# Attention ahead of an MoE and an MLP on one core: another order of issue, second-batch logits in column groups, a mask matmul of 96 columns

## The chip, the cores and the metric

One core of one Trainium2 chip runs the whole program in one launch. The metric is device time in microseconds (us); the time before is the median of three runs. Engines are named as the profile names them: PE (TensorE matmul), PEld (its weight loads), DVE (VectorE), ACT (ScalarE), POOL (GpSimd), SP (SyncE, which issues the loads and stores).

## The reference, cut to what matters

```
B, H, S, D = 2, 8, 768, 64;  block, window = 32, 16;  nb = 24
k_sum = max over each 32 keys;  v_sum = mean over each 32 values
scores = [ q k^T / 8, masked to |i - j| < 16 ;  q k_sum^T / 8 + log(32) ]      # 768 + 24 columns
x = softmax(scores) @ [v ; v_sum]                      # -> x: 1536 tokens x 512
logits = x @ w_gate                                    # 8 experts, 192 tokens each, greedy by the largest logit
out[tokens of e] = relu(x[tokens of e] @ w1[e]) @ w2[e]
h = out @ w_in;  result = relu(h)^2 @ w_out
```

## The kernel before

The program has two parts. `attention` (lines 61 to 413) computes x and the router's logits, and it also does the first round of the routing; `moe` (from line 588) does the other seven rounds, the eight experts and the MLP.

**Units.** Attention is cut into twelve units of four (head pair, 128 query tokens) slots. Units 0 to 5 are the first batch; the four slots of a unit are four neighbouring blocks there. Units 6 to 11 are the second batch: a unit is one block of 128 tokens with all four head pairs, so that the 512 features of its tokens are complete. Each unit passes through the same steps: `sc` (two mask matmuls that write a PSUM tile `S` through the identity, L246, and sixteen score matmuls on 64 x 64 pieces of the array, L250), `sm` (row maximum, DVE, L259), `sb` (exponentials, ACT, L263), `tr` (PE transposes of the probabilities, L270, and the copy of them), `pv` (sixteen matmuls with the values, L284), `pn` (division by the sum, DVE, L294 to L299), `st` (store of x), `xt` (PE transposes of x, L321, and the copy), `la` and `lb` (logits, below). Ahead of the units stand, for each batch and head pair, the steps `lk`, `lq`, `lv` (loads), `rk`, `rq` (copies of rows), `pk`, `pq` (PE transposes, L193, with the copy), `pb` and `pw` (block maxima and key windows), and `va`, `vb`, `vc` (sums of the values; L110 and L119 on PE).

**Logits.** In the first batch `la` issues four matmuls, one into each group of 32 columns of the array (L342: 32 weight columns, 128 moving columns each), ACT copies the result (`lt`, L345), and `lb` adds the four groups with one full matmul (L353). In the second batch `la` accumulates four full matmuls with x as the weights and 8 moving columns (L336), DVE copies the 8 columns to `L9` (L337), and there is no `lb`.

**Routing in attention.** `to`, `ro`, `ch` take the largest logit of some blocks, transpose it into a row and make the one-hot choice; `g` compares (DVE, L562, 36 of them, 256 to 1536 columns wide), and `cn` counts with matmuls on 32 columns of the array (L574). `cl` is the last count and `cd` reads the result (L583, L585). The first instruction of `moe` on PE is the transpose at L734; after it come matmuls on the identity that nobody reads (L676), then L772.

**What sets the order.** Every step is a token of the table `ORDER` (lines 31 to 54), and line 410 walks through it: a token's instructions are put at the end of the lists of their engines. Each engine works through its own list in that order and waits where an operand is not there. A last digit 0, 1 or 2 in `rk`, `rq`, `pk`, `pq`, `tr`, `xt`, `vc`, `pw` names the engine that copies (ACT, DVE, POOL). `w.n` issues n matmuls of 512 columns on the identity that nobody reads (L370). All PE steps but `sc`, `pv` and `cn` write tiles `T` of one pool of three PSUM buffers, so the fourth `T` waits for the copy of the first.

**Form of the array.** A PE instruction uses the full array (L193, L246, L270, L321, L336, L353, L370, L526), 64 x 64 pieces (L250), 64 columns (L284) or 32 columns (L110, L119, L342, L574). "A change of form" below is a neighbouring pair of PE instructions with different forms.

Of the kernel before, what the change touches and what calls it, by code (L numbers as in the profile page):

```python
# [25 lines left out]
WIN = 96  # L26
KW = WIN + NB
# [1 line left out]

PART = ((0, 6), (6, 8), (8, 10), (10, 12))  # L30
ORDER = """
w.8 rk.0.0.0 pk.0.0.0.0 lk.0.3 rk.0.1.1 rq.0.0.1 pk.0.0.1.0 w.2 pk.0.1.0.0 pq.0.0.0.0 lq.1.3 pb.0.0 rq.0.1.1
pw.0.0.2 lq.0.2 pk.0.1.1.0 pq.0.0.1.1 sc.0 lk.0.2 pb.0.1 rk.0.3.2 sm.0.0 rq.1.3.0 pq.0.1.0.1 lv.0.0 sm.0.1
pk.0.3.0.1 pk.0.3.1.1 pq.1.3.0.1 pw.0.1.2 rq.0.2.2 sb.0.0 w.2 sc.1 rk.0.2.2 sm.1.0 pq.0.1.1.1 sb.0.1 sb.1.0 tr.0.1.0
pq.1.3.1.0 pb.0.3 sm.1.1 lk.1.0 pk.0.2.0.0 pw.0.3.2 sc.2 sb.1.1 sm.2.1 lk.1.2 tr.0.0.1 lq.0.3 pk.0.2.1.0 tr.1.0.0
sm.2.0 pb.0.2 sb.2.0 tr.1.1.1 rk.1.0.1 pq.0.2.0.0 va.0.0 pq.0.2.1.1 sb.2.1 pw.0.2.2 rq.0.3.2 lq.1.1 tr.2.0.1 vb.0.0
pk.1.0.0.1 lk.1.3 rk.1.2.0 vc.0.0.0.1 sc.3 lq.1.0 lk.1.1 rq.1.1.2 vc.0.0.1.1 tr.2.1.0 sm.3.0 sm.3.1 pk.1.0.1.0
pq.0.3.0.1 sb.3.0 rq.1.0.2 pb.1.0 pv.0 pk.1.2.0.0 rk.1.3.2 pn.0 lv.0.1 lq.1.2 sb.3.1 pk.1.2.1.1 sc.4 pq.1.1.0.0
tr.3.1.0 sm.4.0 sm.4.1 sb.4.0 pv.1 rk.1.1.2 pw.1.0.2 pq.0.3.1.0 pq.1.1.1.0 lw pk.1.1.0.0 sc.5 pk.1.1.1.0 pn.1 pb.1.2
sm.5.1 pw.1.2.2 pq.1.0.0.1 xt.0.1 sm.5.0 sb.4.1 pk.1.3.0.0 pk.1.3.1.0 pv.2 pb.1.1 pb.1.3 xt.1.0 st.1 pw.1.3.2 sb.5.0  # L40
tr.4.1.1 va.0.1 la.0 la.1 rq.1.2.1 pq.1.2.0.0 pn.2 st.0 pw.1.1.2 lb.0 vb.0.1 vc.0.1.1.2 lb.1 vc.0.1.0.1 tr.3.0.0
lv.1.0 lv.1.1 sb.5.1 xt.2.1 sc.6 la.2 sm.6.0 st.2 sb.6.0 tr.5.1.0 tr.4.0.0 lb.2 pv.3 pn.3 sc.7 sm.7.0 xt.3.1
tr.5.0.1 sb.7.0 va.1.0 sm.6.1 la.3 pv.5 lb.3 pn.5 sb.6.1 sm.7.1 pq.1.2.1.0 st.5 pq.1.0.1.1 sc.8 op xt.5.1 sb.7.1
sm.8.0 pv.4 sb.8.0 tr.6.1.1 la.5 pn.4 va.1.1 lb.5 vb.1.0 sm.8.1 vb.1.1 tr.6.0.0 xt.4.1 vc.1.1.0.1 sc.9 sb.8.1 sm.9.0
st.3 la.4 tr.7.0.0 sm.9.1 vc.1.0.0.2 tr.8.0.0 lb.4 pv.6 sb.9.0 to.0 pn.6 vc.1.0.1.2 st.4 vc.1.1.1.2 ro.0 tr.7.1.0
ch.0.0 st.6 sb.9.1 sc.10 pv.7 ch.0.1 ch.0.2 ch.0.3 xt.6.0 g.0.0 g.0.1 cn.0 tr.8.1.0 g.0.2 tr.9.1.0 sm.10.1 pn.7
g.0.3 la.6 sm.10.0 xt.7.0 sb.10.0 g.0.4 pv.8 tr.9.0.0 pn.8 la.7 cn.1 sb.10.1 g.0.5 to.1 tr.10.0.0 ch.1.0 ch.1.1 pv.9
pn.9 ro.1 st.7 sc.11 g.1.0 g.1.1 sm.11.0 xt.9.0 xt.8.0 tr.10.1.0 cn.2 sm.11.1 g.1.2 sb.11.1 g.1.3 g.1.4 la.9 g.1.5
sb.11.0 g.1.6 cn.3 la.8 pv.10 cn.4 ch.1.2 to.2 ch.1.3 st.8 ro.2 pn.10 tr.11.1.0 cn.5 tr.11.0.0 st.9 cn.6 g.1.7
ch.2.0 xt.10.0 g.2.0 cn.7 g.2.1 cn.8 g.2.2 pv.11 g.2.3 pn.11 la.10 st.10 ch.2.1 g.2.4 cn.9 g.2.5 g.2.6 cn.10 g.2.7  # L50
xt.11.0 cn.11 g.2.8 la.11 cn.12 ch.2.2 cn.13 cn.14 to.3 ro.3 cn.15 cn.16 cn.17 g.2.9 cn.18 ch.2.3 g.3.0 cn.19 g.3.1
cn.20 g.3.2 ch.3.0 ch.3.1 cn.21 qu g.3.3 g.3.4 g.3.5 cn.22 g.3.6 cn.23 cn.24 ch.3.2 cn.25 cn.26 cn.27 g.3.7 g.3.8
ch.3.3 g.3.9 st.11 cn.28 cn.29 cn.30 cn.31 g.3.10 cn.32 cn.33 cn.34 g.3.11 cl cd
"""


# [4 lines left out]
def attention(ctx, tc, nc, q, k, v, wg, x_dram, L9, identf, identb, late=None):  # L61

    const = ctx.enter_context(tc.tile_pool(name="a_const", bufs=1))
# [1059 lines left out]
```

## Time and profile before

| | us |
|---|---|
| median of three runs (603.37 to 604.30) | 603.57 |
| the profiled execution, its own time | 604.21 |
| its span on the core | 602.2 |
| busy in the span: PE / DVE / ACT / POOL | 584.5 / 357.5 / 194.3 / 79.9 |
| attention: first mask matmul on PE to the end of `cd` | 11.58 to 106.65 |

A row of the timeline gives the start, the busy time of a merged run of instructions, the engine, the line, the operands, the count and, in brackets, the idle time ahead of it and what ended it. Busy time of PE overlaps between neighbours, so the cost of a group of matmuls is read as the distance from its start to the next group's start. A matmul on float32 operands leaves two records, a transpose one. PEclk is the granted clock of PE, 1.00 for 2.4 GHz and 0.50 for 1.2 GHz.

### The profile page before, as it was taken

What the parts mean: (1) busy time and instruction counts of PE and PEld (TensorE: products, weight loads), DVE (VectorE), ACT (ScalarE), POOL (GpSimd) and SP (SyncE); (2) the same over time, 40 slices, a digit from 0 to 9 for tenths busy, and PEclk for the clock granted to TensorE, in tenths of its full rate; (3) what the DMA queues carried; (4) which work ended last, traced back from release to release, by engine and by line L of the source; (5) the groups of instructions that cost most, each with busy time, mean ns of one, the idle gap of its engine ahead of it and who ended that gap; (6) DMA issues with size and microseconds to landing.
All of it is one profiled execution on the core that took longest, in us unless ns stands there. A gap on an engine that the chain in (4) does not pass through costs nothing.

```text
span 602.2 us, 10554 instructions
## 1 busy us (share of the span) xinstructions
PE 584.5 (97%) x4118; PEld 479.5 (80%) x4118; DVE 357.5 (59%) x830; ACT 194.3 (32%) x416; POOL 79.9 (13%) x132
## 2 busy tenths in 40 slices
PE   6999998899999999999999999999999999999996
PEld 4677785478879788799999888888888888888884
DVE  6896867679888797955566688873322222322221
ACT  4775663213223142312222333332312222222221
POOL 7354300202030220211000000000300000300002
PEclk8999988899999999999999999999999999999998
DMA  9995111452726548269853254320100000100001
GB/s 242 246 201 113 55 53 38 165 212 94 282 83 227 208 150 289 91 224 308 307 200 115 96 174 136 130 86 0 71 0 2 1 0 1 70 2 0 1 0 70
DMA packets 55393, 71.34 MB, mean 118 GB/s; under 512 B 21296, under 2 KB 32560, under 8 KB 55344
## 3 DMA queue, kind: packets, MB, share of 16 engines
q1 hardware_dynamic: 53360, 64.38, 33.9%
q0 software_dynamic: 1984, 6.29, 3.1%
q8 instruction: 32, 0.52, 0.4%
q14 instruction: 17, 0.14, 0.1%
HBM read 64.37 MB, written 6.29 MB: 117 GB/s over the span
## 4 chain that ended last, share of the span: by engine, by line
PE 79%; issue 13%; DVE 3%; DMA 2%; POOL 1%; ACT 1%; SPq 0%; POOLq 0%; DVEq 0%; ACTq 0%
PE pg L1023 16%; PE ph L919 15%; PE ph L936 15%; PE ph L1049 11%; PE px L1049 4%; PE cnt L574 3%; PE O L284 2%; PE T L193 2%; PE T L270 2%; PE S L250 2%; POOL out_dram L1059 1%; PE ms L526 1%; DMA rawk<-in_k_dram 1%; PE T L321 1%; PE T L110 1%
## 5 line engine op out<-in xcount | busy, mean ns | idle before, releaser
L919 PE MATMUL ph<-xt,w 128*128 128x192 f32 x512 | 92.2, 332 | 0.0
L936 PE MATMUL ph<-ht,w 128*128 128x192 f32 x512 | 91.4, 331 | 0.0
L936 PEld LDWEIGHTS ph<-ht,w 128*128 128x128 f32 x512 | 82.6, 190 | 6.8 <-issue 6.7
L562 DVE TENSOR_SCALAR G<-mrow,m 128x1536 bf16<-128x1536 f32 (+4 forms) x108 | 84.5, 836 | 4.9 <-PE cnt L574 2.7
L919 PEld LDWEIGHTS ph<-xt,w 128*128 128x128 f32 x512 | 82.4, 190 | 5.0 <-issue 4.3
L1023 PE MATMUL pg<-yhi,w 128*128 128x512 f32 x192 | 59.4, 391 | 0.0
L1027 DVE TENSOR_TENSOR xa<-xa 128x512 f32<-128x512 f32 x24 | 16.6, 692 | 58.2 <-ACT xa L1026 57.7
L1027 DVE TENSOR_TENSOR xb<-xb 128x512 f32<-128x512 f32 x24 | 16.6, 691 | 54.4 <-ACT xb L1026 54.4
L1059 POOL DMA_INDIRECT out_dram<-f,sci x6 | 5.9, 979 | 301.5 <-DVE f L1057 300.9
L1023 PEld LDWEIGHTS pg<-yhi,w 128*128 128x128 f32 x192 | 36.1, 188 | 7.7
L1023 PE MATMUL pg<-ylo,w 128*128 128x512 f32 x96 | 37.5, 391 | 0.0
L1049 PE MATMUL ph<-w,xt 128*128 128x512 f32 x144 | 35.3, 389 | 0.0
L1026 ACT ACTIVATE xa<-pg 128x512 f32<-128x512 f32 x24 | 14.2, 592 | 59.3 <-PE pg L1023 59.3
L924 ACT ACTIVATE ht<-ph 128x384 f32<-128x384 f32 x32 | 15.7, 491 | 52.7 <-PE ph L919 50.4
L1026 ACT ACTIVATE xb<-pg 128x512 f32<-128x512 f32 x24 | 14.2, 594 | 55.7 <-PE pg L1023 55.7
L1049 PEld LDWEIGHTS ph<-w,xt 128*128 128x128 f32 x144 | 27.0, 188 | 5.6
L1023 PE MATMUL pg<-yhi,w2b 128*128 128x512 f32 x96 | 30.2, 395 | 0.0
L1023 PE MATMUL pg<-yhi,w2a 128*128 128x512 f32 x96 | 29.7, 391 | 0.0
L263 ACT ACTIVATE P<-S,nm 128x120 f32<-128x120 f32 x96 | 26.6, 372 | 8.8 <-DVE nm L259 8.3
L631 DVE TENSOR_SCALAR f<-raw 128x512 int32<-128x512 int32 x32 | 13.5, 423 | 18.6 <-DMA raw<-in_moe_w_in_dram 10.7
L942 ACT ACTIVATE yhi<-ph 128x384 fp32r<-128x384 f32 x16 | 7.8, 488 | 51.3 <-PE ph L936 40.9
L635 DVE SCALAR_TENSOR_TENSOR f<-raw,f 128x512 int32<-128x512 int32 x32 | 22.2, 693 | 1.0
(234 smaller groups left out, 1005.0 us busy)
## 6 DMA issues: line engine op xcount, KB each, us to landing
w<-in_moe_w_dram SPq DMA_DIRECT2D x64, 512.0 KB, 6.0
raw<-in_moe_w_in_dram SPq DMA_DIRECT2D x16, 512.0 KB, 3.7
raw<-in_moe_w_out_dram SPq DMA_DIRECT2D x16, 512.0 KB, 3.2
vw<-in_v_dram SPq DMA_DIRECT2D x16, 240.0 KB, 5.6
rawk<-in_k_dram SPq DMA_DIRECT2D x8, 384.0 KB, 7.0
rawq<-in_q_dram SPq DMA_DIRECT2D x8, 384.0 KB, 7.1
x_dram<-x SPq DMA_DIRECT2D x10, 256.0 KB, 2.2
vw<-in_v_dram SPq DMA_DIRECT2D x8, 80.0 KB, 4.8
```

The source lines that it names most:

```text
L263: nc.scalar.activation(P[u][:, hh, i], SS[u][hh][:, i], AF.Exp, bias=NM[u][:, hh, i:i + 1])
L562: self.nc.vector.tensor_scalar(t[:, used:used + w], self.mrow[:, 128 * j0:128 * j1], self.m[:, c:c + 1], CS, op0=OP.is_le, op1=OP.mult)
L574: self.nc.tensor.matmul(self.cnt[32 * g:32 * g + 32, 128 * (lo - 3 * g):128 * (hi - 3 * g)], self.o[:, c, :], t[:, 128 * (lo - j0):128 * ( ...
L631: nc.vector.tensor_scalar(fi, raw[:, :, 1], 3, 0x3FFFFFF8, op0=OP.logical_shift_left, op1=OP.bitwise_and)
L635: nc.vector.scalar_tensor_tensor(fi, raw[:, :, 0], 29, fi, op0=OP.logical_shift_right, op1=OP.bitwise_or)
L919: nc.tensor.matmul(ps[:, j, 0:CAP], w[:, k, 128 * (f % 4):128 * (f % 4) + 128], d["xt"][:, k, :], start=(k == 0), stop=(k == 3), skip_grou ...
L924: nc.scalar.activation(d["ht"][:, f0:f0 + 2, :], ps[:, :, 0:CAP], AF.Relu)
L936: nc.tensor.matmul(ps[:, j, 0:CAP], w[:, f % 4, 128 * dd:128 * dd + 128], d["ht"][:, f, :], start=(f == 0), stop=(f == 7), skip_group_chec ...
L1023: nc.tensor.matmul(ps, a[:, k, fs], b[:, k, js], start=(n == 0), stop=(n == 11))
L1026: nc.scalar.activation(r, ps, AF.Relu)
L1027: nc.vector.tensor_tensor(r, r, r, op=OP.mult)
L1049: nc.tensor.matmul(PO[j][t], a[:, 128 * t:128 * t + 128], b[:, f % 4, :], start=(f == 0 and n == 0), stop=(f == 15 and n == 2))
```

## The change

The order table is replaced. It has the same tokens but for these: six `lb` are added (units 6 to 11), the fillers `w` go from 8, 2, 2 to 8, 2, 3, 3, 3, 3, 4, and 42 of the tokens with an engine digit copy on another engine. The second batch's `la` becomes that of the first batch, and a new branch in `lb` sums the four groups into 8 columns with one full matmul. The mask loses its last 24 columns, which were zero, and the mask matmul writes 4 x 96 columns of S where it wrote 480.

```diff
-w.8 rk.0.0.0 pk.0.0.0.0 lk.0.3 rk.0.1.1 rq.0.0.1 pk.0.0.1.0 w.2 pk.0.1.0.0 pq.0.0.0.0 lq.1.3 pb.0.0 rq.0.1.1
...
+w.8 rq.0.0.1 rk.0.0.0 lq.0.2 pk.0.0.0.0 pk.0.0.1.1 lk.0.2 rk.0.1.0 pb.0.0 lk.0.3 w.2 pq.0.0.0.0 w.3 pk.0.1.0.0
...
-    mask = const.tile([128, 12, KW], BF, name="mask")
-    nc.vector.tensor_copy(mask, ma[:, None, :].to_broadcast([128, 12, KW]))
+    mask = const.tile([128, 12, WIN], BF, name="mask")
+    nc.vector.tensor_copy(mask, ma[:, None, :].to_broadcast([128, 12, WIN]))
...
-            m = mask[:, c:c + 1, :].to_broadcast([128, 4, KW])
+            m = mask[:, c:c + 1, :].to_broadcast([128, 4, WIN])
...
-            nc.tensor.matmul(ss[hh], identb, m, start=True, stop=False, skip_group_check=True)
+            nc.tensor.matmul(ss[hh][:, :, 0:WIN], identb, m, start=True, stop=False, skip_group_check=True)
...
-        if b == 1:
-
-            ps = pT.tile([128, E], F32, name="T")
-            for a in range(4):
-                nc.tensor.matmul(ps, xt[:, a, :], wgs[:, a, 0:E], start=a == 0, stop=a == 3)
-            nc.vector.tensor_copy(L9[:, 6 + slots[0][1], 0:E], ps)
-            return
...
         ps = pT.tile([128, 4, E], F32, name="T")
+        if b == 1:
+
+            nc.tensor.matmul(ps[:, 0, :], lt, esel24[:, 0:E], start=True, stop=True)
+            nc.vector.tensor_copy(L9[:, 6 + slots[0][1], 0:E], ps[:, 0, :])
+            return
```

Line numbers of the changed kernel are one higher between the order table and the mask and two lower from the second part of `logit_b` on. Three places show how the lists move.

On PE in the second batch, before: the end of a unit's probabilities (`P`), logits (L336), the next unit's x, its values (`O`) and its logits.

```order
L270 MATMUL T<-identf,P 120x128 x8
L336 MATMUL T<-wgs,xt 128x8 x4
L321 MATMUL T<-identf,x 128x128 x4
L284 MATMUL O<-vw,PT 64x65 x16
L270 MATMUL T<-identf,P 120x128 x4
L336 MATMUL T<-wgs,xt 128x8 x4
```

The same two units (6 and 7) in the changed kernel, where L335 is the first half of the logits, L348 the second half, and L246 and L250 the scores of the last unit.

```order
L321 MATMUL T<-identf,x 128x128 x4
L284 MATMUL O<-vw,PT 64x65 x16
L335 MATMUL T<-xt,wgs 32x128 x8
L270 MATMUL T<-identf,P 120x128 x4
L246 LDWEIGHTS identb
L246 MATMUL S<-mask,identb 128x4x96
L246 LDWEIGHTS identb
L246 MATMUL S<-mask,identb 128x4x96
L250 MATMUL S<-kw,qt 64x120 x16
L348 MATMUL T<-esel_165,lt 128x8 x2
L284 MATMUL O<-vw,PT 64x65 x16
```

Two units' logits stand side by side now, their second halves six groups later, between groups of the same form.

On DVE at the start, before: the first rows of k and q (`rk`, `rq`), then the block maxima `ks` of the first head pair.

```order
L184 COPY rk<-rawk 128x768
L184 COPY rq<-rawq 128x768
L209 TENSOR_REDUCE ks<-kt_107 128x24
L184 COPY rq<-rawq 128x768
L226 TENSOR_SCALAR qt<-T 128x384
```

In the changed kernel the q rows of the first head pair come first and the copy of its keys follows; the k rows of the second head pair are copied on ACT.

```order
L184 COPY rq<-rawq 128x768
L202 COPY kt_107<-T 128x384
L209 TENSOR_REDUCE ks<-kt_107 128x24
L202 COPY kt_108<-T 128x384
L209 TENSOR_REDUCE ks<-kt_108 128x24
```

The first block maxima no longer stand behind two copies of rows, the first of which needs the third load.

On PE at the end of attention, before: the last count (L574), the transpose that opens `moe` (L734) and its first filler.

```order
L574 LDWEIGHTS O_0_1103
L574 MATMUL S<-G,O_0_1103 32x384
L734 MATMUL ms<-identf,tm 128x128
L676 LDWEIGHTS identb
L676 MATMUL ph<-identb 128x512
```

The same place in the changed kernel.

```order
L572 LDWEIGHTS O_0_1240
L572 MATMUL S<-G,O_0_1240 32x384
L368 LDWEIGHTS identb
L368 MATMUL T<-identb 128x512
L368 LDWEIGHTS identb
L368 MATMUL T<-identb 128x512
L368 LDWEIGHTS identb
L368 MATMUL T<-identb 128x512
L368 LDWEIGHTS identb
L368 MATMUL T<-identb 128x512
L732 MATMUL ms<-identf,tm 128x128
```

Four fillers (`w.4`) stand between the last count and the transpose; three more groups of three stand among the counts ahead of them. From L588 on (the part `moe`) the lists of all five engines are the same in both kernels.

## Rows read from the trace of the kernel before

**Rows 1.** Four stretches: length; busy us of PE, PEld, DVE, ACT, POOL; PEclk; DMA share; GB/s

```profile
12.00:87.00 75.00, 71.75 (x1148) 54.78 (x1146) 60.52 (x132) 49.51 (x150) 28.17 (x43) 1.00 0.66 141
87.00:91.00 4.00, 4.00 (x44) 3.16 (x43) 2.33 (x12) 0.95 (x4) 0.20 (x1) 0.57 0.01 2
98.00:107.00 9.00, 6.04 (x50) 2.67 (x45) 7.15 (x21) 2.34 (x5) 0.45 (x2) 0.69 0.00 0
107.00:111.00 4.00, 4.00 (x13) 1.53 (x12) 2.10 (x14) 0.00 (x0) 0.00 (x0) 0.50 0.19 55
```

**Rows 2.** Timeline of PE: logits by full matmuls (L336), and the clock's fall

```profile
75.60 0.96 PE L336 MATMUL T<-wgs,xt 128*128 128x8 f32 x8
76.41 0.63 PE L321 MATMUL T<-identf,x 128*128 128x128 f32 x4
...
86.11 1.06 PE L336 MATMUL T<-wgs,xt 128*128 128x8 f32 x8
87.09 1.95 PE L284 MATMUL O<-vw,PT 120*64 120x65 f32 x32
```

**Rows 3.** Timeline of PE: transposes, the logits in column groups (L342, L353), values

```profile
48.75 0.43 PE L342 MATMUL T<-xt,wgs 128*32 128x128 f32 x8 [0.97 <-DVE xt L324]
49.11 1.09 PE L270 MATMUL T<-identf,P 128*120 128x128 f32 x8
50.03 0.31 PE L353 MATMUL T<-esel,lt 128*128 128x32 f32 x2
50.27 1.15 PE L284 MATMUL O<-vw,PT 120*64 120x65 f32 x32
```

**Rows 4.** Timeline of ACT in the second batch: exponentials (L263) and what stands behind them

```profile
85.32 2.13 ACT L263 ACTIVATE P<-S,nm 128x120 f32<-128x120 f32 x8
90.14 0.39 ACT L529 ACTIVATE mrow<-T 128x256 f32<-128x256 f32 x1 [2.69 <-PE T L526]
```

**Rows 5.** Timeline of PE and DVE at the opening of `moe`

```profile
106.98 3.19 PE L676 MATMUL ph<-identb 128*128 128x512 bf16 x7
109.96 0.23 PE L772 MATMUL ms<-sel,low 128*128 128x24 bf16 x1
...
108.53 0.23 DVE L765 SCALAR_TENSOR_TENSOR sel<-m,m,os 128x12 bf16<-128x12 f32 x1
```

**Rows 6.** Timeline of PE: two groups of one form, then a change of form

```profile
28.59 0.49 PE L193 MATMUL T<-identf,rk 128*128 128x128 f32 x3
28.92 0.49 PE L193 MATMUL T<-identf,rq 128*128 128x128 f32 x3
29.34 1.15 PE L284 MATMUL O<-vw,PT 120*64 120x65 f32 x32
```

**Rows 7.** Timeline of PE at the start

```profile
8.99 0.87 PE L193 MATMUL T<-identf,rk 128*128 128x128 f32 x3 [2.32 <-DVE rk L184]
...
11.58 0.83 PE L246 MATMUL S<-mask,identb 128*128 128x480 bf16 x2
```

**Rows 8.** The loads of the second half of the first batch's values, and their use

```profile
32.57 1.17 SPq L99 DMA_DIRECT2D vw<-in_v_dram  x1
...
41.56 1.51 PE L110 MATMUL T<-vw,own 96*32 96x256 f32 x24
...
vw<-in_v_dram SPq DMA_DIRECT2D x16, 240.0 KB, 5.6
```

**Rows 9.** Timeline of PE and DVE from the last logits to the end of `cd`

```profile
97.58 0.82 PE L574 MATMUL S<-G,O 128*32 128x384 bf16 x8
...
98.46 0.89 DVE L562 TENSOR_SCALAR G<-mrow,m 128x1280 bf16<-128x1280 f32 x1 [0.40 <-PE S L574]
...
99.79 0.88 DVE L562 TENSOR_SCALAR G<-mrow,m 128x256 bf16<-128x256 f32 x3 [0.36 <-PE S L574]
...
102.62 2.21 DVE L562 TENSOR_SCALAR G<-mrow,m 128x256 bf16<-128x256 f32 x3
105.51 0.56 DVE L583 SCALAR_TENSOR_TENSOR mg<-S,mg 128x384 f32<-128x384 f32 x1 [0.68 <-PE S L574]
```

More of the change, by code (lines that the diff above doesn't have):

```diff
@@ L31 @@
 ORDER = """
-w.8 rk.0.0.0 pk.0.0.0.0 lk.0.3 rk.0.1.1 rq.0.0.1 pk.0.0.1.0 w.2 pk.0.1.0.0 pq.0.0.0.0 lq.1.3 pb.0.0 rq.0.1.1
[L33 to L51, printed above, removed]
@@ L52 @@
-cn.20 g.3.2 ch.3.0 ch.3.1 cn.21 qu g.3.3 g.3.4 g.3.5 cn.22 g.3.6 cn.23 cn.24 ch.3.2 cn.25 cn.26 cn.27 g.3.7 g.3.8
-ch.3.3 g.3.9 st.11 cn.28 cn.29 cn.30 cn.31 g.3.10 cn.32 cn.33 cn.34 g.3.11 cl cd
+w.8 rq.0.0.1 rk.0.0.0 lq.0.2 pk.0.0.0.0 pk.0.0.1.1 lk.0.2 rk.0.1.0 pb.0.0 lk.0.3 w.2 pq.0.0.0.0 w.3 pk.0.1.0.0
+pw.0.0.2 pq.0.0.1.0 lv.0.0 rq.0.2.0 rq.0.1.0 pk.0.1.1.1 rk.0.2.2 sc.0 pb.0.1 sm.0.0 pw.0.1.2 pq.0.2.0.0 pq.0.1.0.1
+sm.0.1 sb.0.0 pq.0.1.1.0 lq.0.3 sb.0.1 lk.1.1 pk.0.2.0.1 pk.0.2.1.1 pb.0.2 sc.1 lk.1.3 sm.1.0 sm.1.1 rk.0.3.2
@@ new lines @@
+pk.0.3.0.0 sb.1.0 pw.0.2.1 lk.1.2 pk.0.3.1.1 tr.0.1.0 tr.0.0.1 sc.2 rq.0.3.2 sm.2.0 sm.2.1 sb.1.1 sb.2.0 tr.1.0.1
+tr.1.1.0 va.0.0 lw pb.0.3 pq.0.2.1.1 tr.2.0.1 lq.1.2 vb.0.0 lq.1.0 pq.0.3.0.0 vc.0.0.1.1 rk.1.1.2 sb.2.1 sc.3
+vc.0.0.0.2 sm.3.0 sm.3.1 sb.3.0 lk.1.0 pk.1.1.0.1 rk.1.2.2 pv.0 pw.0.3.2 sb.3.1 tr.2.1.0 rq.1.0.2 pk.1.1.1.1
+pk.1.2.0.0 rk.1.3.0 pn.0 lv.0.1 pb.1.1 sc.4 pq.0.3.1.1 sm.4.0 xt.0.0 pk.1.2.1.0 lq.1.3 pv.1 pn.1 lq.1.1 la.0
+pw.1.1.2 pq.1.0.0.0 tr.3.0.1 rk.1.0.2 sb.4.0 tr.3.1.0 lb.0 rq.1.2.1 pv.2 sm.4.1 pb.1.2 pk.1.0.0.0 xt.1.0 pk.1.0.1.1
@@ new lines @@
+st.0 pn.2 sb.4.1 pb.1.0 sc.5 la.1 va.0.1 sm.5.0 sb.5.0 pw.1.2.2 lb.1 pq.1.0.1.1 lv.1.0 st.1 pw.1.0.2 pk.1.3.0.1
+xt.2.0 vb.0.1 pk.1.3.1.0 vc.0.1.1.1 pq.1.2.0.0 lv.1.1 rq.1.3.2 la.2 pq.1.3.0.0 tr.4.0.0 tr.5.0.0 rq.1.1.2 lb.2
+vc.0.1.0.2 pb.1.3 pv.3 pq.1.1.0.0 sm.5.1 pn.3 pw.1.3.2 st.3 sb.5.1 tr.4.1.0 sc.6 xt.3.0 pv.4 sm.6.0 sm.6.1 sb.6.0
+st.2 la.3 pn.4 tr.5.1.1 tr.6.0.0 lb.3 sc.7 sm.7.0 sb.7.0 xt.4.1 pq.1.3.1.0 pq.1.1.1.1 sb.6.1 pv.5 sm.7.1 tr.7.0.0
+pq.1.2.1.1 sb.7.1 va.1.0 va.1.1 pn.5 la.4 vb.1.0 vb.1.1 lb.4 vc.1.1.0.1 tr.7.1.0 xt.5.0 sc.8 sm.8.0 la.5 sm.8.1 st.5
@@ new lines @@
+sb.8.0 vc.1.0.0.2 pv.7 lb.5 pn.7 op st.4 vc.1.1.1.2 tr.6.1.0 to.0 sc.9 ch.0.0 ch.0.1 sb.8.1 ch.0.2 pv.6 sm.9.0
+sm.9.1 pn.6 st.6 tr.8.0.1 sb.9.0 ro.0 sb.9.1 sc.10 tr.8.1.0 xt.7.0 g.0.0 tr.9.0.0 g.0.1 ch.0.3 g.0.2 sm.10.0 sm.10.1
+xt.6.0 g.0.3 pv.8 g.0.4 st.7 pn.8 sb.10.0 la.7 vc.1.0.1.2 la.6 g.0.5 tr.9.1.0 sc.11 sb.10.1 st.8 sm.11.0 lb.7 lb.6
+to.1 pv.9 sm.11.1 sb.11.0 pn.9 ro.1 ch.1.0 g.1.0 tr.10.1.0 xt.8.0 tr.10.0.0 ch.1.1 xt.9.0 g.1.1 tr.11.0.0 sb.11.1
+cn.0 g.1.2 g.1.3 pv.10 g.1.4 ch.1.2 g.1.5 la.8 cn.1 la.9 cn.2 tr.11.1.0 g.1.6 pn.10 lb.8 lb.9 cn.3 g.1.7 to.2 ch.1.3
@@ L54 @@
+ch.2.0 ch.2.1 pv.11 pn.11 cn.4 ro.2 g.2.0 cn.5 g.2.1 g.2.2 xt.10.0 cn.6 xt.11.0 ch.2.2 g.2.3 cn.7 la.10 g.2.4 cn.8
+g.2.5 cn.9 la.11 cn.10 g.2.6 lb.10 g.2.7 cn.11 lb.11 ch.2.3 to.3 g.2.8 cn.12 cn.13 st.11 w.3 cn.14 ro.3 ch.3.0 g.2.9
+cn.15 st.10 g.3.0 cn.16 cn.17 ch.3.1 g.3.1 cn.18 cn.19 cn.20 g.3.2 cn.21 g.3.3 w.3 cn.22 cn.23 cn.24 g.3.4 g.3.5
+cn.25 g.3.6 g.3.7 g.3.8 g.3.9 cn.26 ch.3.2 cn.27 qu cn.28 w.3 cn.29 cn.30 g.3.10 ch.3.3 cn.31 cn.32 cn.33 cn.34
+g.3.11 cl st.9 w.4 cd
 """
@@ L127, in vsum_c @@
             VP[b, g][WIN:KW, :, None, :].to_broadcast([NB, 4, 6, D]))
-    jq = const.tile([128, KW], I32, name="jq")
-    nc.gpsimd.iota(jq, pattern=[[1, KW]], base=0, channel_multiplier=-1)
+    jq = const.tile([128, WIN], I32, name="jq")
+    nc.gpsimd.iota(jq, pattern=[[1, WIN]], base=0, channel_multiplier=-1)
     bi = const.tile([96, 54], I32, name="bi")
@@ L145, in attention @@
             new_v(b, g)
-    jf = const.tile([128, KW], F32, name="jf")
-    ma = const.tile([128, KW], F32, name="ma")
-    mb = const.tile([128, KW], F32, name="mb")
+    jf = const.tile([128, WIN], F32, name="jf")
+    ma = const.tile([128, WIN], F32, name="ma")
+    mb = const.tile([128, WIN], F32, name="mb")
     nc.vector.tensor_copy(jf, jq)
@@ L154, in attention @@
     nc.vector.tensor_tensor(ma, ma, mb, op=OP.min)
-    nc.vector.memset(ma[:, WIN:], 0.0)
-    mask = const.tile([128, 12, KW], BF, name="mask")
-    nc.vector.tensor_copy(mask, ma[:, None, :].to_broadcast([128, 12, KW]))
+    mask = const.tile([128, 12, WIN], BF, name="mask")
+    nc.vector.tensor_copy(mask, ma[:, None, :].to_broadcast([128, 12, WIN]))
     for i in (0, 6):
```

## The prediction

> **What bounds the kernel now.** I read the busy table first: PE is busy for 97% of the span. Busy PE need not be PE at its pace, so the stretches come next [rows 1]. From 12 to 87 us PE stands still for only 75.00 - 71.75 = 3.25 us, while DVE works for 60.5 of the 75 and ACT for 49.5: PE's own list sets the pace, and DVE is the nearest behind it. From 98 to 107 it is the other way round: DVE works for 7.2 of 9 us, PE for 6.0, and DVE's comparisons lead to `cd`. Then I looked at the clock, which is 0.57 in 87 to 91, 0.69 in 98 to 107 and 0.50 in 107 to 111: PE works at half speed there for a part of the time. From `moe` on the lists are the same and PE is nearly always busy, so whatever attention and the opening of the routing gain or lose is carried to the end. The sum is made against the profiled execution's own 604.2, of which 2.0 lie outside the span and stay. The median of the runs shown is 0.6 lower.
>
> **The change, part by part.** Between the first mask matmul and the last logits both lists hold the same PE work except for four items.
>
> Logits of the second batch, six units. Four full matmuls now cost 0.81 us (75.60 to 76.41) where the same form follows and 0.98 (86.11 to 87.09) where another does [rows 2]. The first half in column groups costs 0.36 (48.75 to 49.11) with a change of form at its end, so some 0.26 without, and the second half 0.24 (50.03 to 50.27) [rows 3]. A unit goes from 0.81 to 0.50, at most from 0.98 to 0.50: 1.9 to 2.9 us for six. I take 2.1, near the lower end, since changes of form are counted apart. The new copy on ACT and the handover to it are costed at nothing: ACT stands still for 2.7 us in one piece there [rows 4], and PE has two to six other groups between the halves. Without that cover it would be a wait per unit, a rival below.
>
> The mask. A filler of 512 columns takes 2.98 / 7 = 0.43 us at half clock [rows 5], so 0.21 at full clock, and 96 columns are 0.04. For 24 matmuls that is 1.0 us; it would be 0 if something other than the columns set the time of these matmuls. They stand alone ahead of the scores, so I take 1.0.
>
> Changes of form. Counted in the lists from the first mask to the last logits they go from 80 to 73. A group of three transposes takes 0.33 us ahead of another of its form (28.59 to 28.92) and 0.42 ahead of the values (28.92 to 29.34) [rows 6]: a change costs 0.09, and seven fewer give 0.7 with 0.1 each; 0 if the distance has another cause. The Trainium skill (TensorEngine Tiling (Array Packing), Key Properties) says that a change of tiling mode drains the engine, which speaks against logits in column groups; taking the fixed part of a lone matmul from TensorE: Matmul & The Clock Gate (Single matmul latency), 398 cycles or 0.17 us, as an estimate of the drain, the seven would give 1.2 and the two changes that a lone first half needs would cost 0.33, most of the unit's gain. The trace's 0.09 decides.
>
> Fillers up to there: two fewer, 0.4 at most, and nothing where they only filled a wait. I take 0.2.
>
> The clock from 87 to 91. At 0.57 for 4 us some 1.7 us of full speed are lost, and the values at 87.09 show it: 1.95 us busy [rows 2] against 1.15 [rows 6]. Ahead of the fall PE ran two of the full logits groups, whose matmuls move 8 columns each [rows 2]. These groups are gone, so I take 1.6 as regained; 0 if the clock falls all the same.
>
> The start. PE waited 2.32 us for the k rows of the second head pair, did the transposes behind them at half clock (0.87 us busy against 0.49) and reached the first mask at 11.58 [rows 6, 7]. In the new list the block maxima of the first head pair no longer stand behind these rows, the copy of the q rows comes first, and PE has q transposes and three fillers to do in between. The load itself comes no sooner. From nothing (same load, clock still low) to 1.3 (full clock, windows ready): I take 0.7.
>
> Waits. If PE's work shrinks by 4 us, not every wait of 12 to 87 stays as it is. DVE is at 81%, and one load has no slack: the last piece of the first batch's second values is issued by 32.57 + 1.17, lands 5.6 us later at 39.3 and is used at 41.56 [rows 8]. The new order has eighteen transposes fewer ahead of that use (0.11 each), twelve smaller mask matmuls (0.5) and two first halves, one second half and a filler more (0.9): 1.6 us less, and with the start's 0.7 the use would come at 39.3 as well. From 0 more to a doubling of the 3.25; I take half of that, 1.5.
>
> The tail. From the end of the last logits (97.58) to the end of `cd` (106.65) it takes 9.1 us, with DVE waits of 0.40, 0.36 and 0.68 for PE [rows 9]. In the new order one more 1280-wide comparison stands behind the last logits. DVE's list there: copy, one-hot and maximum 0.5; two of 1280 columns, 1.8; ten of 256 at 0.29, 2.9; four short ones of the choice, 0.7; two of 1536 at (2.21 - 0.29) / 2, 1.9; the wait for the last count 0.7; `cd` 1.1. That is 9.6: 0.5 longer. The nine fillers ahead of the last count (1.9 us at full clock) lie beside this, as PE works only 6 of 9 us there.
>
> The opening of the routing. Seven fillers took 106.98 to 109.96 at half clock, and L772 behind them waited for them alone, since its operand was there at 108.53 + 0.23 = 108.76 [rows 5]. At full clock they end at 108.5, and L772 follows its operand: 1.2 us sooner. The new fillers among the counts and behind the last one keep PE at work where it stood still. From 0 to 1.5 (some of the next fillers too); I take 1.0.
>
> Sum: -2.1 - 1.0 - 0.7 - 0.2 - 1.6 - 0.7 + 1.5 + 0.5 - 1.0 = -5.3, so 598.9 for an execution like the profiled one and 598.3 for the median of runs.
>
> **The rivals.**
>
> The clock does not stay up. Terms of 1.6 and 1.0 fall away: 600.9. For it: it fell at 87 although PE was busy in all of it [rows 1], and the tail still has pauses. The new list also puts six groups of transposes in a row behind the values of unit 9. The Trainium skill (TensorE: Matmul & The Clock Gate, Part 4) says that transposes do not count as a busy PE, by which such a run would bring the fall back, again 600.9; the trace does not decide it, as the transposes at 8.99 came behind 2.3 us of idle time and those at 28.59 ran at full clock.
>
> The work saved on PE turns into waits. If the 4.0 of logits, mask, form and fillers all go there, 4.0 - 1.5 more than the sum allows are lost: 600.8. For it: DVE's 81% and the load without slack; against it: PE had only 3.25 us of waits with much the same DVE list.
>
> No change: the loads and DVE, not PE, pace the first 50 us, and the tail's DVE list takes the rest, so PE's smaller list ends in the same place: 603.6. Against it stands the 96% of PE in 12 to 87.
>
> Slower: the logits' new copy on ACT. The tile `T` of a first half is now freed by ACT, which takes it in turn behind exponentials of up to 2.13 us [rows 4], and with three `T` the fourth transposes or logits behind it stop PE. One first half already waited 0.97 us for a copy [rows 3]. The whole gain is gone at 5.3 / 6 = 0.9 us per unit; at 1.2 per unit it is 598.3 + 7.2 = 605.5. Against it: ACT works two thirds of the time, and less in the last units.
>
> **How the numbers follow.** Chances: the forecast 0.50, the clock 0.20, waits 0.15, no change 0.07, slower 0.08. The predicted time is the forecast's 598.3. Its own range goes down to the ends of the bounds that are most open (waits 1.5, logits 0.8, start 0.6 less: 595.4) and up to 599.8. The two rivals next to it end at 601; with 0.6 for their own spread the range is 595.3 to 601.6, which leaves out the last two and little else. A measurement tells this kernel from no change at about 0.2%, 1.2 us. So faster has 0.50 + 0.20 + 0.15 = 0.85, same 0.07, slower 0.08.
>
> **What would show it.** In the profile after: no group of full logits, first halves of 0.24 to 0.36 and second halves of 0.24; pairs of mask matmuls 0.08 shorter; the first scores under a microsecond sooner; PE's idle time between the first mask and the last logits below 5 us; a clock of 1.00 from 75 us to the last logits; `cd` ending near 102.4 instead of 106.65; the seven fillers of the routing's opening in 1.5 us instead of 3. I am wrong if DVE or a load holds PE for long in the first 50 us, if the clock falls in the tail, or if transposes wait for `T` behind the exponentials.

## The result, and the profile after

The changed kernel takes 594.25 us (median of 4 runs, 594.06 to 594.66). The kernel before, run beside it, takes 603.93 (603.37 to 605.07). The ratio is 0.9846 with a 95% interval of 0.9825 to 0.9868. It is faster, as forecast, but by 9.7 us where 5.3 were forecast, and 594.25 lies below the range. Two disturbed runs of experiments (972.13 and 1157.79 us) are left out of every comparison.

Stretches of the changed kernel: first mask matmul to last logits, from there to the transpose that opens `moe`, from there to L770 (L772 before); then two stretches that answer to the cold ones of [rows 1]. Columns as there.

```profile
10.75:88.32 77.57, 75.80 (x1268) 58.35 (x1265) 61.85 (x155) 56.34 (x166) 30.65 (x45) 1.00 0.70 150
88.32:97.24 8.92, 7.16 (x64) 2.90 (x64) 7.99 (x24) 2.35 (x5) 1.81 (x2) 1.00 0.01 2
97.24:99.16 1.92, 1.80 (x8) 0.81 (x9) 1.36 (x8) 0.00 (x0) 0.00 (x0) 1.00 0.00 0
...
87.00:91.00 4.00, 3.99 (x44) 2.15 (x44) 3.00 (x12) 1.25 (x5) 0.90 (x1) 1.00 0.27 104
97.00:101.00 4.00, 3.65 (x19) 1.73 (x20) 3.06 (x21) 0.00 (x0) 0.00 (x0) 1.00 0.04 12
```

The first of these stretches in the kernel before, which [rows 1] does not hold in one piece:

```profile
11.58:97.58 86.00, 82.21 (x1257) 62.73 (x1255) 67.24 (x157) 52.93 (x157) 28.76 (x45) 0.98 0.60 131
```

PE's busy time fell by 6.41 us and its waits from 86.00 - 82.21 = 3.79 to 77.57 - 75.80 = 1.77. DVE fell by 5.4 us; ACT rose by 3.4 and POOL by 1.9. The clock is 1.00 in all of these stretches. What PE waited for in the new stretch (total us, times, longest):

```profile
PE O L284 <- POOL vw L126: 0.7, 2, 0.5
PE S L246 <- ACT P L263: 0.6, 2, 0.4
```

Timeline of PE and DVE in the changed kernel: the start, a mask pair, transposes in a row, logits, the opening of the routing.

```profile
9.66 0.55 PE L193 MATMUL T<-identf,rk 128*128 128x128 f32 x3 [0.71 <-ACT rk L186]
...
10.75 0.49 PE L246 MATMUL S<-mask,identb 128*128 128x384 bf16 x2
...
77.43 0.60 PE L321 MATMUL T<-identf,x 128*128 128x128 f32 x4
77.87 0.60 PE L270 MATMUL T<-identf,P 128*120 128x128 f32 x4
...
78.78 0.65 PE L270 MATMUL T<-identf,P 128*120 128x128 f32 x4
...
80.72 0.43 PE L335 MATMUL T<-xt,wgs 128*32 128x128 f32 x8
80.96 0.33 PE L572 MATMUL S<-G,O 128*32 128x384 bf16 x2
...
87.47 0.39 PE L348 MATMUL T<-esel,lt 128*128 128x8 f32 x2
87.79 0.28 PE L572 MATMUL S<-G,O 128*32 128x256 bf16 x1
...
95.95 0.56 DVE L581 SCALAR_TENSOR_TENSOR mg<-S,mg 128x384 f32<-128x384 f32 x1 [0.52 <-PE S L572]
96.54 0.55 DVE L583 TENSOR_REDUCE tm<-mg 128x1 f32<-128x384 f32 x1
97.24 0.29 PE L732 MATMUL ms<-identf,tm 128*128 128x128 f32 x1 [0.44 <-DVE tm L583]
97.37 1.67 PE L674 MATMUL ph<-identb 128*128 128x512 bf16 x7
99.16 0.17 PE L770 MATMUL ms<-sel,low 128*128 128x24 bf16 x1
```

A first half of the logits costs 80.96 - 80.72 = 0.24, with the same form behind it, and a second half 87.79 - 87.47 = 0.32, with a change of form behind it. From the transpose that opens `moe` to L770, with seven fillers between them, it takes 1.92 us where 109.96 - 106.71 = 3.25 stood before.

The spans add up, read from the two profiled executions. The start gives 0.83 us, the stretch to the last logits 8.43, the tail 0.21 (9.13 to 8.92), the opening 1.33, and the way from L770 to the first expert matmul 0.35 (12.47 to 12.12); the rest of the program takes 0.25 more. Together -10.9, from a span of 602.2 to 591.3. In the profiled execution 3.4 us lay outside the span where 2.0 did before; in the other three it was 2.2 to 2.4, with spans of 591.7 to 592.1.

### The profile page after: what moved, and what is told of

It reads as the page before. It is cut to its first block, busy times and chain, and to the rows that moved or that the text cites. A ratio compares the mean times of both kernels' runs of the same rounds, so it can differ in the third digit from the quotient of the medians.

```text
span 591.3 us, 10618 instructions
## 1 busy us (share of the span) xinstructions
PE 578.3 (98%) x4144; PEld 474.5 (80%) x4144; DVE 352.0 (60%) x826; ACT 197.5 (33%) x425; POOL 81.5 (14%) x132
## 4 chain that ended last, share of the span: by engine, by line
PE 76%; issue 14%; POOL 5%; DVE 2%; DMA 2%; ACT 1%; POOLq 0%; SPq 0%; ACTq 0%; DVEq 0%
PE pg L1021 16%; PE ph L934 15%; PE ph L917 15%; PE ph L1047 11%; PE px L1047 4%; PE cnt L572 3%; PE O L284 2%; PE T L270 1%; POOL out_dram L1057 1%; PE S L250 1%; PE ms L524 1%; PE T L193 1%; POOL vw L126 1%; PE T L111 1%; PE T L321 1%
## 5 line engine op out<-in xcount | busy, mean ns | idle before, releaser
L263 ACT ACTIVATE P<-S,nm 128x120 f32<-128x120 f32 x96 | 26.9, 378 | 4.5 <-DVE nm L259 4.1
```

The source lines that it names most:

```text
L263: nc.scalar.activation(P[u][:, hh, i], SS[u][hh][:, i], AF.Exp, bias=NM[u][:, hh, i:i + 1])
```

## The experiments

"Old" means the kernel before, "new" the changed one, from which the others start but for the two with the old order or sequence. The table gives the median time and, of the profiled execution, its own time and, from the first mask matmul to the last logits, PE's and DVE's busy time, PE's waits (length minus busy) and the clock. Where the two times differ, the columns behind them belong to the profiled one. Before was timed beside them at 603.18, 603.71 and 603.27 (medians of 17, 21 and 9 runs).

| kernel | time | profiled | PE busy | PE waits | DVE busy | clock |
|---|---|---|---|---|---|---|
| before | 603.93 | 604.21 | 82.21 | 3.79 | 67.24 | 0.98 |
| changed | 594.25 | 594.66 | 75.80 | 1.77 | 61.85 | 1.00 |
| full logits | 599.96 | 596.84 | 78.36 | 2.69 | 61.09 | 1.00 |
| full logits, second profile | 601.82 | 601.82 | 83.41 | 1.95 | 61.17 | 0.93 |
| mask of 120 columns | 594.11 | 593.95 | 76.76 | 1.39 | 61.99 | 1.00 |
| no fillers in the tail | 595.09 | 595.09 | 75.89 | 2.00 | 61.92 | 1.00 |
| old order, new code | 602.51 | 602.67 | 79.37 | 6.93 | 67.49 | 0.98 |
| new sequence, old engines | 602.97 | 606.27 | 81.60 | 8.94 | 65.99 | 0.94 |
| old sequence, new engines | 606.7 | 605.62 | 81.78 | 6.12 | 63.17 | 1.00 |
| old engines for keys and queries | 598.06 | 596.73 | 76.12 | 5.40 | 61.52 | 1.00 |
| old engines for the rest | 600.72 | 600.86 | 79.33 | 5.98 | 66.46 | 0.96 |
| two value sums on DVE | 594.84 | 596.12 | 76.22 | 2.79 | 63.81 | 1.00 |

**Full logits in the second batch again.**

```diff
+        if b == 1:
+            ps = pT.tile([128, E], F32, name="T")
+            for a in range(4):
+                nc.tensor.matmul(ps, xt[:, a, :], wgs[:, a, 0:E], start=a == 0, stop=a == 3)
+            nc.vector.tensor_copy(L9[:, 6 + slots[0][1], 0:E], ps)
+            return
...
+        if b == 1:
+            return
```

> The changed kernel, but the second batch's logits again as four full matmuls copied by DVE; its lb tokens then issue nothing. Theory (the new order brings the gain, the logits a share of it): PE work between the first mask and the last logits grows by 6 x (0.86 - 0.50) = 2.2 us, PE's waits there stay near 1.8 us, the clock stays at 1.00; time 594.3 + 2 to 2.5 = 596.5. Rival 1 (matmuls with 8 moving columns are what brought the clock down): the same and a stretch below 1.00 between 70 and 95 us, 1.5 to 2 us more, 598.3. Rival 2 (the logits are hidden): 594.3.

Measured: 599.96 (596.84 to 601.23, 7 runs), ratio 0.9942 [0.9925, 0.9959]. The profiled execution was the fastest: it kept the full clock, with 78.36 - 75.80 = 2.56 us more PE work. The other six took 2.5 to 4.4 us longer, at a mean clock of 0.989 to 0.995 where the profiled one had 0.997. So the same kernel was profiled once more.

> The same kernel as with the full logits in the second batch, for one more profile. Its profiled execution had the full clock all through attention and took 596.8, six others took 599.3 to 601.2. Theory that the full logits bring the clock down in most executions: a time near 600 and a granted clock below 0.7 for some 3 us or more behind a unit's full logits (L336), as before the change at 87 to 91. Rival, that the loss of the other six lies elsewhere (the start or the tail): full clock behind the logits, and the clock below 1.00 there.

Measured: 601.82. Stretches of this execution:

```profile
76.00:80.00 4.00, 4.00 (x58) 3.28 (x56) 3.30 (x14) 4.00 (x12) 0.00 (x0) 1.00 0.00 0
80.00:84.00 4.00, 4.00 (x38) 3.10 (x32) 1.50 (x6) 0.81 (x4) 0.00 (x0) 0.84 0.00 0
84.00:88.00 4.00, 3.63 (x40) 2.33 (x38) 2.82 (x11) 0.73 (x2) 0.20 (x1) 0.50 0.01 4
...
96.00:100.00 4.00, 4.00 (x25) 1.57 (x24) 2.64 (x8) 1.67 (x4) 0.84 (x1) 0.52 0.00 0
```

Its timeline of PE where the clock falls:

```profile
80.24 1.06 PE L335 MATMUL T<-wgs,xt 128*128 128x8 f32 x8
81.23 0.34 PE L579 MATMUL S<-G,O 128*32 128x384 bf16 x2
81.50 1.06 PE L335 MATMUL T<-wgs,xt 128*128 128x8 f32 x8
82.49 0.34 PE L579 MATMUL S<-G,O 128*32 128x384 bf16 x2
82.76 1.11 PE L270 MATMUL T<-identf,P 128*120 128x128 f32 x4
```

The four transposes at 82.76 take 1.11 us, against 0.65 in the changed kernel at 78.78: half clock, right behind two groups of full logits, in a stretch in which PE never stood still. The kernel before, too, fell behind full logits [rows 2]. Of the four profiles with full logits (before, the two here, and the old sequence with new engines) two fall there and two stay at 1.00; the ten with column groups, all the others, stay at 1.00 from 60 us to the last logits. So the theory holds as a count: the column groups give back the clock besides their own work, though not every execution loses it without them. What in these groups brings it down is not shown: six groups of transposes in a row (76.10 to 78.89) stand ahead of them in this execution, and it lost more than any of the six that it stands for.

**A mask of 120 columns again** (the constants as wide as before).

```diff
-            nc.tensor.matmul(ss[hh][:, :, 0:WIN], identb, m, start=True, stop=False, skip_group_check=True)
+            nc.tensor.matmul(ss[hh], identb, m, start=True, stop=False, skip_group_check=True)
```

> The changed kernel with the mask of 120 columns again, so that a mask matmul writes 480 columns. Theory (columns set the time of a mask matmul and PE sets the pace): a pair of mask matmuls goes from 0.42 to 0.50 us, twelve pairs 1.0 us, time 595.2. Rival (hidden in PE's waits): the pairs longer, the last logits no later, 594.3.

Measured: 594.11 (593.95 to 595.1), ratio 0.9843 [0.9824, 0.9862]. PE does 0.96 us more, 0.04 for each of 24 matmuls as computed; 0.38 of it fills waits, the stretch to the last logits is 0.58 longer, and the whole can't be told from the changed kernel's 594.06 to 594.66. In the time the rival came out and not the theory's 595.2.

**No fillers in the tail** (all `w` behind `to.3` removed).

```diff
-cn.11 lb.11 ch.2.3 to.3 g.2.8 cn.12 cn.13 st.11 w.3 cn.14 ro.3 ch.3.0 g.2.9
+cn.11 lb.11 ch.2.3 to.3 g.2.8 cn.12 cn.13 st.11 cn.14 ro.3 ch.3.0 g.2.9
...
-g.3.11 cl st.9 w.4 cd
+... g.3.11 cl st.9 cd
```

> The changed kernel without the thirteen fillers behind the last top (three groups of three and the four at the end). Theory (the fillers hold the clock): the granted clock falls below 1.00 in the tail or in the first 4 us of the routing, the seven fillers of the routing's opening take 2 to 3 us instead of 1.8, time 594.3 + 0.8 to 1.4 = 595.4. Rival (the clock stays up because the new order has no slow stretch ahead of the tail): the clock stays at 1.00 and the time at 594.3, or 0.2 less since DVE waits less for PE in the tail.

Measured: 595.09 (594.24 to 595.34), ratio 0.985 [0.9831, 0.9869]. Its tail and opening:

```profile
88.34:97.11 8.77, 5.32 (x51) 2.04 (x51) 7.90 (x23) 2.35 (x5) 1.80 (x2) 0.86 0.01 2
97.11:100.37 3.26, 3.26 (x9) 1.27 (x10) 1.36 (x8) 0.00 (x0) 0.00 (x0) 0.50 0.01 3
```

The fillers cost the tail 0.15 us and give 1.34 in the opening; 0.84 is left in the medians, though two of its five runs (594.24 and 594.4) lie among the changed kernel's. The thirteen together are what keeps the clock there; which of them it needs was not tried.

**The old order with the new code** (mask of 96 columns, column groups; the six new `lb` put where I chose, units later than their `la`).

```diff
-... pv.8 ... g.0.5 ... cn.3 ... cn.4 ... cn.10 ... cn.14 ...
+... pv.8 lb.6 ... g.0.5 lb.7 ... cn.3 lb.9 ... cn.4 lb.8 ... cn.10 lb.10 ... cn.14 lb.11 ...
```

> The old order table with the mask of 96 columns and the logits of the second batch in column groups; the six new lb stand two or three PE groups behind their la. Theory (waits and clock belong to the order, the two edits only shorten PE's list): PE work down by 2.2 + 1.0, waits between the first mask and the last logits stay near 3.8 us, the fall of the clock at 87 us is gone (1.6); time 603.9 - 3.2 to -4.8 = 599.1 to 600.7. Rival (the edits bring nearly all of it, whatever the order): 595 to 597. Rival (without the new order the extra copy and the extra T stop PE): 603 or more.

Measured: 602.51 (600.29 to 603.86, 12 runs), ratio 0.9988 [0.9967, 1.0008]. PE's waits from the first mask matmul to the last logits, the longest four:

```profile
PE T L347 <- ACT lt L337: 2.0, 3, 1.4
PE T L334 <- DVE xt L323: 1.1, 1, 1.1
PE T L523 <- DVE den L293: 0.9, 1, 0.9
PE T L334 <- ACT xt L325: 0.5, 1, 0.5
```

PE does 2.84 us less and waits 3.14 us more. In this order the rival "the work saved on PE turns into waits" came true, and 2.0 us of it stands behind the new copy `lt` on ACT, as the slower rival feared. These 2.0 depend on where I put the six `lb`; other places were not tried. The clock did not fall at 87 us here: it is 1.00 from 16 us to the last logits.

**The new sequence with the old copy engines, and the reverse** (the 42 digits exchanged between the two tables).

```diff
-w.8 rq.0.0.1 rk.0.0.0 lq.0.2 pk.0.0.0.0 pk.0.0.1.1 lk.0.2 rk.0.1.0 pb.0.0 ...
+w.8 rq.0.0.1 rk.0.0.0 lq.0.2 pk.0.0.0.0 pk.0.0.1.0 lk.0.2 rk.0.1.1 pb.0.0 ...
```

> The changed kernel, but each of the 42 tokens whose copying engine was changed copies on its old engine again; the sequence of the tokens is the new one. Theory (the waits went because the sequence and the engines were chosen together): PE's waits between the first mask and the last logits rise from 1.8 to 4 to 7 us, time 594.3 + 2 to 5. Rival 1 (the sequence alone makes the difference): 594 to 595. Rival 2 (the engines alone make it, DVE having 5 us less to do): back to the waits of the old order, 7 us or more, 599 to 600.

> The kernel before with nothing changed but the engines of the 42 tokens, which are those of the new table. Theory (chosen together): no gain, waits of 4 us or more, 602.5 to 605. Rival 2 (the engines alone make the difference): DVE's busy time in the stretch falls by 5 us, PE's waits from 3.8 to about 2, 601 to 602.

Measured: new sequence with old engines 602.97 (601.72 to 606.27, 11 runs), ratio 0.9997 [0.9976, 1.0018]; old sequence with new engines 606.7 (604.79 to 610.06, 10 runs), ratio 1.0063 [1.0036, 1.009]. PE's waits with the new sequence and old engines, the longest five:

```profile
PE O L284 <- DVE vw L126: 2.4, 2, 1.7
PE T L270 <- DVE kt L202: 2.0, 1, 2.0
PE S L246 <- ACT P L263: 1.3, 1, 1.3
PE T L193 <- ACT rq L186: 1.0, 1, 1.0
PE T L193 <- ACT rk L186: 0.9, 1, 0.9
```

The profiled execution is the slowest of its eleven and lost the clock twice on the way (0.94 in the stretch). Five others had a mean clock of 0.998 or 0.999, the changed kernel's or better, and still took 601.72 to 602.97: 7.5 to 8.7 us more than the changed kernel with no more loss of clock. The second wait of the list shows how one comes about. ACT, DVE and PE there:

```profile
11.68 2.21 ACT L263 ACTIVATE P<-S,nm 128x120 f32<-128x120 f32 x8
13.77 0.89 ACT L204 ACTIVATE kt<-T 128x384 f32<-128x384 f32 x2
14.77 0.95 DVE L209 TENSOR_REDUCE ks<-kt 128x24 f32<-128x768 f32 x1 [1.56 <-ACT kt L204]
...
16.77 1.01 DVE L202 COPY kt<-T 128x384 f32<-128x384 f32 x2
17.38 0.66 PE L270 MATMUL T<-identf,P 128*120 128x128 f32 x4 [1.99 <-DVE kt L202]
```

The keys of the third head pair stand on ACT behind exponentials, DVE stands still for 1.56 us until they are copied, and its own copies of the next keys, for which PE waits, come behind that. In the changed kernel DVE copies these keys itself and goes on without a pause:

```profile
14.44 1.02 DVE L202 COPY kt<-T 128x384 f32<-128x384 f32 x2
15.57 0.95 DVE L209 TENSOR_REDUCE ks<-kt 128x24 f32<-128x768 f32 x1
```

Neither half gives anything alone: without the engines the whole gain of 9.7 us is gone, and the engines without the sequence cost 0.6%, with waits of 6.12 where the kernel before has 3.79. The new engines in the old sequence were run with the old code alone, not with the column groups.

**The engine digits by parts**: the old ones for keys and queries (`rk`, `rq`, `pk`, `pq`, `pw`, 27 digits), or for probabilities, x and value sums (`tr`, `xt`, `vc`, 15 digits).

```diff
-... rq.0.0.1 rk.0.0.0 lq.0.2 pk.0.0.0.0 pk.0.0.1.1 lk.0.2 rk.0.1.0 ...
+... rq.0.0.1 rk.0.0.0 lq.0.2 pk.0.0.0.0 pk.0.0.1.0 lk.0.2 rk.0.1.1 ...
```

```diff
-tr.1.1.0 va.0.0 lw pb.0.3 pq.0.2.1.1 tr.2.0.1 lq.1.2 vb.0.0 lq.1.0 pq.0.3.0.0 vc.0.0.1.1 rk.1.1.2 sb.2.1 sc.3
-vc.0.0.0.2 ...
+tr.1.1.1 va.0.0 lw pb.0.3 pq.0.2.1.1 tr.2.0.1 lq.1.2 vb.0.0 lq.1.0 pq.0.3.0.0 vc.0.0.1.1 rk.1.1.2 sb.2.1 sc.3
+vc.0.0.0.1 ...
```

> The new sequence with the old copy engines for the rows, transposes and windows of keys and queries (27 of the 42 changed digits). In the kernel with all 42 digits old PE waited 8.9 us between the first mask and the last logits, against 1.8 in the changed kernel, and 3.9 of its waits (keys 2.0, q rows 1.0, k rows 0.9) belong to these 27. Theory that the loss adds up by parts: waits of 1.8 + 3.9 = 5.7 us, time 594.3 + 3.9 = 598.2, up to 601 if the clock falls behind the longest wait. Rival, that the first 50 us set everything, so that these 27 carry the whole loss: waits of 8 to 9 us and 602 to 603. Rival, that only the two sets together lose: within 1 us of 594.3.

> The new sequence with the old copy engines for the probabilities, x and the value sums (the other 15 digits). Of the 8.9 us of waits with all 42 old, 4.3 belong to these (value sums 2.4, probabilities 1.3, x 0.6). Theory that the loss adds up by parts: waits of 1.8 + 4.3 - 0.7 = 5.4 us (the 0.7 is the wait for value sums on POOL, which goes), time 594.3 + 3.6 = 597.9. Rival, that keys and queries carry the whole loss: within 1 us of 594.3. Rival, that these carry it: 602 to 603.

Measured: keys and queries 598.06 (596.73 to 598.42), ratio 0.9923 [0.9905, 0.994], waits 5.40; the rest 600.72 (599.13 to 601.19), ratio 0.996 [0.994, 0.998], waits 5.98. The totals of the first are what the sum by parts said (598.2, 5.7), in part by luck: the k rows on ACT now cost 1.6 us where 0.9 was summed, the keys 1.4 where 2.0 was. The second has nearly the waits of the sum (5.4), but 1.6 us of them for q rows on POOL, which are none of its fifteen digits, and 2.8 us more time than the sum. Its timeline of PE shows why:

```profile
41.47 0.43 PE L335 MATMUL T<-xt,wgs 128*32 128x128 f32 x8
43.48 0.55 PE L193 MATMUL T<-identf,rq 128*128 128x128 f32 x3 [1.58 <-POOL rq L184]
43.87 1.53 PE L270 MATMUL T<-identf,P 128*120 128x128 f32 x8
...
47.27 2.00 PE L284 MATMUL O<-vw,PT 120*64 120x65 f32 x32 [1.60 <-DVE vw L126]
```

The clock falls behind the first wait, ahead of the second, and the values behind that take 2.00 us busy instead of 1.15: the clock is 0.53 from 44 to 48 and 0.61 from 48 to 52, and PE is busy for 3.5 us more in the stretch than in the changed kernel. A wait alone does not settle it: with the old engines for keys and queries PE stands still for 1.65 us ahead of 30.39, and the clock stays at 1.00. The two sets of digits cost 3.8 and 6.5 us; together they lose 8.7, a little less than their sum of 10.3.

**Two value sums on DVE.**

```diff
-vc.0.0.0.2 ... vc.0.1.0.2
+vc.0.0.0.1 ... vc.0.1.0.1
```

> The changed kernel with two of its value sums copied on DVE instead of POOL (vc.0.0.0 and vc.0.1.0, the old digits). The largest wait left in the changed kernel is values behind these copies on POOL, 0.7 us in two pieces. Theory that a wait can be taken out by itself: waits of 1.1 us, time 593.6. Rival, that DVE, at 80% in this stretch, hands the time on to another wait: 594.3 or up to 1 us more, with a wait of PE on DVE of 0.5 us or longer that the changed kernel doesn't have.

Measured: 593.94, 594.84 and 596.12. The wait for the value sums did not go: it is 1.3 us in one piece, now behind DVE, and one of 0.5 for rows on POOL is new (2.79 in all). The rival holds, and this is no better version.

**What a change of form costs**: 32 matmuls on the identity in the middle of attention (between `pq.1.3.1.0` and `pq.1.1.1.1`), 16 on the full array and 16 on 32 columns, first grouped, then in turn (`[full, part] * n`).

```diff
+        full = lambda: nc.tensor.matmul(s[:, 0, :], identb, identb, start=True, stop=True, skip_group_check=True)
+        part = lambda: nc.tensor.matmul(s[0:32, 1, :], identb[:, 0:32], identb, start=True, stop=True,
+                                        skip_group_check=True)
+        for f in [full] * n + [part] * n:
+            f()
```

> The changed kernel with 32 additional matmuls of 128 columns that nobody reads in the middle of attention: sixteen on the full array, then sixteen on 32 columns of it. Only the distance from the first of them to the next group on PE is of interest: with two or three changes of form, some 32 x 0.06 = 1.8 us. It is the base for the next kernel, which issues the same 32 in turn.

> The same 32 matmuls, issued full, part, full, part: 30 changes of form more. With 0.09 us a change, as read from the trace of before, the distance grows by 2.7 us; if a change drains the engine at the estimated 0.17, by 5; if a change costs nothing of itself, by less than 0.5.

Measured: 594.37 grouped and 598.99 in turn, one run each. Grouped:

```profile
52.06 1.06 PE L365 MATMUL T<-identb 128*128 128x128 bf16 x16
53.05 1.07 PE L366 MATMUL T<-identb 128*32 128x128 bf16 x16
54.05 0.55 PE L193 MATMUL T<-identf,rq 128*128 128x128 f32 x3
```

In turn (the first, the last, and what follows):

```profile
53.35 0.22 PE L365 MATMUL T<-identb 128*128 128x128 bf16 x1
...
58.32 0.23 PE L366 MATMUL T<-identb 128*32 128x128 bf16 x1
58.48 0.55 PE L193 MATMUL T<-identf,rq 128*128 128x128 f32 x3
```

The same work takes 54.05 - 52.06 = 1.99 us grouped and 58.48 - 53.35 = 5.13 in turn. Thirty more changes of form cost 3.14 us, 0.10 each.

## Why the prediction was right and wrong

**The step that failed is the term for waits.** I reasoned that "if PE's work shrinks by 4 us, not every wait of 12 to 87 stays as it is" and added 1.5, from bounds of 0 to 3.25 more that left out any fall. The waits fell by 2.0, from 3.79 to 1.77: an error of 3.5 us, where the forecast of 598.3 missed by 4.05. I had taken DVE's list and the copies behind PE as given ("much the same DVE list") and gave the 42 changed digits no term at all. With the old digits in the new sequence the waits are 8.94 instead of 1.77, and the time is that of before; with the new digits in the old sequence they are 6.12. So the fall comes from the two together, and the term had weighed only PE's shorter list, DVE's load and one transfer. Fifteen of them take DVE from 66.46 to 61.85 us in the stretch. DVE's load is not the whole of it, though: the other 27 leave it as it is (61.52) and still hold 3.6 us of waits, so there it matters what stands ahead of a copy on its engine, as the 1.56 us that DVE stood still behind ACT show. The waits that I feared are real in the other order: with the old one PE's saved 2.84 us came back as 3.14 us of waits, but 2.0 of these stand behind ACT's new copy and not behind DVE's load or a transfer. The load said to have no slack held nothing: its last piece is issued by 32.15 + 1.10 in the changed kernel, and PE uses it at 37.99 without a wait, sooner than the 39.3 of the forecast.

**Logits, right and a little small.** 2.1 were forecast; 2.56 us of PE work come back with the full matmuls. The copy on ACT cost nothing in the new order, as costed.

**The clock, right in its sign and too small.** 1.6 were forecast for 87 to 91, and 1.0 for the opening. With full logits in the new order the other six executions, at lower mean clocks, are 2.5 to 4.4 us slower than the one that keeps the clock. Three executions of the kernel before, timed beside the experiments, had a mean clock of 0.997 and took 599.85 to 600.69: by these, 3.2 to 4.1 us of the 9.7 are the clock, and 5.6 to 6.4 are left with the clock kept. The rival by which a run of transposes brings the fall back did not happen in the changed kernel: six groups stood in a row from 76.72 to 79.36, two of them 77.87 - 77.43 = 0.44 us apart, at a clock of 1.00. What the Trainium skill states of transposes (TensorE: Matmul & The Clock Gate, Part 4) did not show here.

**Changes of form, the price right.** 0.09 was read from [rows 6] and 0.10 was measured. The estimate of 0.17 that I had worked out beside the Trainium skill's draining array (TensorEngine Tiling (Array Packing), Key Properties) is too high here. What the seven fewer give was not tested by itself. The second halves do not stand between groups of the same form, as said of the change: the two of units 6 and 7, at 75.10, stand between scores on 64 x 64 pieces and values on 64 columns. The counts of 80 and 73 hold in the traces.

**The mask, right in PE's work, wrong in time.** 0.96 us of the 1.0 are there, but 0.38 went into waits and nothing of it can be told in the medians.

**The start**: 0.7 forecast, 0.83 seen. The eight other profiles with this same start list reach the first mask at 9.60 to 10.66, ahead of the 10.75 here, so a single profile doesn't settle this term to better than a microsecond.

**Tail and opening.** The tail was forecast 0.5 longer and is 0.2 shorter: I laid DVE's comparisons end to end behind the last logits (9.6), and it is busy for 7.99 of 8.92 us. The opening was forecast at 1.0 and gave 1.33; without the tail's fillers it is 3.26, as before.

Beyond the terms, PE's busy time fell by 6.4 in the stretch where the terms for logits, mask, form, fillers and clock made 5.6; no run separates the other 0.8. What stays open: why the full logits bring the clock down in most executions and not in all, and how far a sequence of the old kind could be improved by other engine digits than the new ones.

## What to carry to other kernels

When a change of order also changes which engine copies, cost the engines first: count what each gains and loses in the stretch and, for each copy that PE waits for, what stands ahead of it on its new engine. A shorter list on the busy engine was worth its length here only with the lists that feed it made anew: the new code gave 0.7 us in the old order (603.18 to 602.51, and 2.0 at the end of its interval), and its logits alone 2.6 to 5.7 in the new one. A wait can be dearer than it looks: the clock fell to half behind one of 1.58 us and stayed there for some 7 us, though it stayed up behind one of 1.65 in another kernel.

## What was not expected of the hardware

The granted clock fell to 0.50 (1.2 GHz) while PE was busy in every microsecond from 76 to 84, right behind two groups of full matmuls of 8 moving columns, and stayed there until about 100 us; the same groups left it at 1.00 (2.4 GHz) in another execution of the same kernel. A change of form at every matmul more than doubled the time of 32 short ones (62 ns to 160 ns each, 128 columns in bf16).
